# W_q in four loads of strided rows and x in two loads, in a decode kernel that streams its K and V caches

## The chip, the cores and the metric

The kernel runs on one core of one Trainium2 chip. The metric is the device time of one execution in microseconds (us). The kernel before takes 659.33 us, the median of 3 runs (659.29 to 659.46).

## What is computed

One decode step of two sequences: a pre-normalised attention block with cached keys and values, and then a gated feed-forward block. All inputs are bf16. Cut to what matters:

```python
B, Sq, D = 2, 1, 512
Hq, Hkv, Sk, Dh = 32, 32, 8192, 128        # F = 1376

def _A_ref(x, k_cache, v_cache, wq, wo):
    q = (x @ wq).reshape(B, Sq, Hq, Dh).transpose(0, 2, 1, 3)
    scores = jnp.einsum("bhqd,bhkd->bhqk", q, k_cache) * (Dh ** -0.5)
    p = _softmax(scores, axis=-1)
    o = jnp.einsum("bhqk,bhkd->bhqd", p, v_cache)
    return o.transpose(0, 2, 1, 3).reshape(B, Sq, Hq * Dh) @ wo

h = x + _A_ref(_layernorm(x), k_cache, v_cache, wq, wo)
h2 = h + _B_ref(_layernorm(h), W_gate, W_up, W_down)
```

K and V are 134 MB each. W_q is 512 x 4096, 4.2 MB. Each x row has 512 values, 1 KB.

## The kernel before

The caches come from HBM as tiles of 128 partitions x 64 KB (8.4 MB). One tile holds four heads of one sequence, with 32 partitions to a head. There are three such buffers (`bufs`). Steps 0 to 14 each take one K tile and one V tile; the last four heads are taken in two steps of half tiles.

A step runs in this order. PE transposes the last 16 to 32 columns of 128 keys (L349) and multiplies them with q (L340). DVE multiplies the rest of the K tile with q (`products`, L375) and adds the products up (`scores`, L393 and L395). ACT takes the exponentials (L415), DVE places them (L420), and PE multiplies them with the V tile (`values`, L446).

The order of all instructions is written out by hand, engine by engine (`tc.manual_schedule`). All large loads are issued by SP, in program order, on one queue; each load into a buffer waits until its old contents have been read. The V tile of step i+1 takes the buffer of step i's K tile, so SP issues it when DVE has finished the scores of step i. The K tile of step i+2 takes the buffer of step i's V tile, so SP issues it when PE has finished its values.

At the start, ACT issues the loads of x (L190) into two partitions of buffer 2, and SP issues W_q (L193) into the first half of the same buffer, where a partition holds four rows of W_q (32 KB). Then SP issues the K and V tiles of step 0 into buffers 0 and 1 (L165, in `load_tile`). Meanwhile POOL fills constants. PE transposes x (L238), `ln_cols` normalises it (L172 to L185), and PE multiplies it with W_q (L252). DVE copies the product into buffer 2 (L255), and PE and ACT spread q over the partitions (L259 to L276). When buffer 2 has been read for the last time (L267), SP issues the K tile of step 1 into it (L279, through L165).

Semaphores of loads are handed out in turn from a set of eight; the loads of x, W_q and the first K and V tile are eight in all.

After the steps come the output projection with W_o (L502 and L509), and the feed-forward block with W_gate and W_up (L686) and W_down (L719). Their loads are the last in SP's queue (L567 to L621), among them three loads of 32 rows of W_down (L616).

Of the kernel before, what the change touches and what calls it, by code (L numbers as in the profile page):

```python
# [13 lines left out]
def _free(t, offset, dims):  # L14

    return bass.AP(tensor=t.tensor, offset=t.offset + offset, ap=[t.ap[0]] + [list(d) for d in dims])


def _dram(t, offset, dims):
    return bass.AP(tensor=t.tensor, offset=t.offset + offset, ap=[list(d) for d in dims])  # L20
# [3 lines left out]
def kernel(  # L24
# [13 lines left out]
    nc = tc.nc  # L38
    P = nc.NUM_PARTITIONS
    B, Sq, D = A_x.shape  # L40
    _, Hkv, Sk, Dh = A_k_cache.shape
    Hq = A_wq.shape[1] // Dh
    F = B_W_gate.shape[1]
    KC = D // P
# [10 lines left out]
    HALF = TILE // 2  # L55
# [36 lines left out]
    bufs = [big.tile([P, TILE], bf16, name=f"tile{k}") for k in range(3)]  # L92
# [67 lines left out]
    def load_tile(cache, s, dst, pieces=1):  # L160
        h = NH * s.g + (0 if s.quad else 2 * s.k)
        n = s.nt * Dh
        w = n // pieces
        for k in range(pieces):
            nc.sync.dma_start(  # L165
                out=dst[:, k * w:(k + 1) * w], in_=_dram(cache, (s.b * Hkv + h) * Sk * Dh + k * w, [[n, P], [1, w]]),
            )

    def ln_cols(src, dst_bkc, pfx):

        m_ps = ps.tile([P, B, KC], f32, tag="mx")
        nc.tensor.matmul(out=m_ps, lhsT=mean_w, rhs=src, start=True, stop=True)  # L172
        mean = small.tile([P, B], f32, tag=pfx + "mean")
        nc.vector.tensor_reduce(out=mean, in_=m_ps, axis=AXIS.X, op=ALU.add)
        dev = small.tile([P, B, KC], f32, tag=pfx + "dev")
        nc.vector.tensor_tensor(out=dev, in0=src, in1=_free(mean, 0, [[1, B], [0, KC]]), op=ALU.subtract)
        sq = small.tile([P, B, KC], f32, tag=pfx + "sq")
        nc.vector.tensor_tensor(out=sq, in0=dev, in1=dev, op=ALU.mult)
        v_ps = ps.tile([P, B, KC], f32, tag="mx")
        nc.tensor.matmul(out=v_ps, lhsT=mean_w, rhs=sq, start=True, stop=True)  # L180
        rstd = small.tile([P, B], f32, tag=pfx + "rstd")
        nc.vector.tensor_reduce(out=rstd, in_=v_ps, axis=AXIS.X, op=ALU.add)
        nc.scalar.activation(out=rstd, in_=rstd, func=ACT.Sqrt, bias=eps_col, scale=1.0)
        nc.vector.reciprocal(out=rstd, in_=rstd)
        nc.vector.tensor_tensor(out=dst_bkc, in0=dev, in1=_free(rstd, 0, [[1, B], [0, KC]]), op=ALU.mult)  # L185

    with tc.manual_schedule():

        for b, k, n in ((0, 0, 2), (0, 2, 2), (1, 0, 2), (1, 2, 1), (1, 3, 1)):
            nc.scalar.dma_start(  # L190
                out=xr[b:b + 1, k * P:(k + n) * P], in_=_dram(A_x, b * D + k * P, [[D, 1], [1, n * P]]),
            )
        nc.sync.dma_start(out=bufs[2][:, 0:HALF], in_=_dram(A_wq, 0, [[KC * Hq * Dh, P], [1, KC * Hq * Dh]]))  # L193
        load_tile(A_k_cache, steps[0], steps[0].kt)
        load_tile(A_v_cache, steps[0], steps[0].vt)

# [5 lines left out]
            out=nscale, in_=nscale, compare_op=ALU.not_equal, fill=-SCALE,  # L202
# [5 lines left out]
            out=ident_f, in_=ident_f, compare_op=ALU.not_equal, fill=1.0,  # L208
# [4 lines left out]
            out=sel, in_=sel, compare_op=ALU.not_equal, fill=1.0,  # L213
# [9 lines left out]
            out=pick, in_=pick, compare_op=ALU.not_equal, fill=1.0,  # L223
# [15 lines left out]
        nc.vector.tensor_copy(xc, x_ps.rearrange("p c b -> p b c"))  # L239
        xn = small.tile([P, KC, B], bf16, tag="xn")  # L240
        ln_cols(xc, xn.rearrange("p c b -> p b c"), "l1")
        for r in SROWS:
            nc.vector.tensor_reduce(out=rest[r], in_=_free(ident, 0, [[1, r], [r, P // r]]), axis=AXIS.X, op=ALU.max)
# [4 lines left out]
        for g0 in range(0, NQ, 4):  # L248
            for n0 in range(NH * g0 * Dh, NH * (g0 + 4) * Dh, 4 * Dh):
                q_ps = ps2.tile([B, 4 * Dh], f32, tag="o")  # L250
                for c in range(KC):
                    nc.tensor.matmul(  # L252
                        out=q_ps, lhsT=xn[:, c, :], rhs=wq_sb[:, c, n0:n0 + 4 * Dh], start=(c == 0), stop=(c == KC - 1),
                    )
                nc.vector.tensor_copy(qrow[:, n0:n0 + 4 * Dh], q_ps)  # L255
            for b in range(B):
                r_ps = ps2.tile([P, 4, Dh], f32, tag="tp")
                for j in range(NH):
                    nc.tensor.matmul(  # L259
                        out=r_ps[j * (P // NH):(j + 1) * (P // NH)], lhsT=sel[:, b, 0:P // NH],  # L260
# [5 lines left out]
        for j in range(2):  # L266
            nc.tensor.matmul(  # L267
                out=r_ps[j * (P // 2):(j + 1) * (P // 2)], lhsT=sel[:, B - 1, :],
# [318 lines left out]
        for k in range(1, len(SETS)):  # L587
# [3 lines left out]
            out=wo[:, (HM + 1) * D:Hq * D], in_=_dram(A_wo, (HM + 1) * Dh * D, [[P // 4 * D, 4], [D, P // 4], [1, D]]),  # L591
# [19 lines left out]
        for w, src in ((0, B_W_gate), (1, B_W_up)):  # L611
            nc.sync.dma_start(
                out=wgu[:, w].rearrange("p c f -> p (c f)"), in_=_dram(src, 0, [[KC * F, P], [1, KC * F]]),
            )
        for q0 in range(AGAIN, P, AGAIN):
            nc.sync.dma_start(  # L616
                out=wd_sb[q0:q0 + AGAIN, FC - 1, :], in_=_dram(B_W_down, (F - P + q0) * D, [[D, AGAIN], [1, D]]),
            )
        for f0, n in FSETS[:-1]:
# [10 lines left out]
            out=z2_ps, lhsT=ones, rhs=_free(zc, ((B - 1) * NQ + groups[Q][1]) * NH, [[1, nb]]), start=True, stop=True,  # L630
# [63 lines left out]
        for c in range(KC):  # L694
            nc.tensor.transpose(hT_ps[:, c, :], hb[:, c].rearrange("p k b -> p (k b)"), ident)
        nc.scalar.activation(
            out=hrow.rearrange("q (p c) -> q p c", c=KC), in_=hT_ps.rearrange("q c p -> q p c"), func=ACT.Copy,
# [9 lines left out]
            out=gate, in0=g_ps, scalar=0.0, in1=_free(rvar, 0, [[0, FC], [1, B]]), op0=ALU.max, op1=ALU.mult,  # L707
# [59 lines left out]
```

## Time and profile before

| | |
|---|---|
| median of 3 runs | 659.33 us (659.29 to 659.46) |
| profiled execution, first to last instruction (span) | 657.5 us |
| busy: PE, DVE, ACT, POOL | 352.1, 558.1, 123.6, 24.1 us |
| moved by DMA | 281.37 MB, mean 428 GB/s |
| x issued, used by PE | 0.74 to 2.38 us, 15.17 us |
| W_q issued, landed | 0.74 us, 12.94 us |
| q: first matmul, last read | 18.56 us, 30.96 us |
| first DVE product of steps 0 and 1 | 32.41 us, 72.48 us |

The profiled execution's own time is known by its span alone; the median of the runs lies 1.8 us above that span. The profile shows 40 equal slices of the span, with the busy share of each engine in tenths. The chain of waits is followed back from the last instruction: each line is a start, a duration and what was waited for. A load in it counts from its issue to its landing, and so includes the time it spent in the queue behind other loads. The trace also holds one record per DMA packet, with its queue, start, duration and size: a row of a tile is one packet, and each DMA engine closes its share of a load with a semaphore packet of 4 bytes. SP's loads are queue 1 and ACT's are queue 10.

### The profile page before, as it was taken

The numbers are of one execution on the slowest core, as the hardware profiler recorded it, in microseconds if no ns is written. First come the engines' busy times: TensorE is split into PE (matmuls) and PEld (weight loads), VectorE is DVE, ScalarE is ACT, GpSimd is POOL, SyncE is SP. The second block draws the span as 40 slices with busy tenths as digits, with TensorE's granted clock in tenths as the row PEclk, the third lists the DMA queues.
The fourth block names the chain that finished last, engine by engine and source line by source line (L and its number), as shares of the span: only waits on it lengthen the run. The fifth ranks groups of instructions, "written<-read, shape, count | busy, mean of one in ns | idle before, by whom it ended". The sixth has DMA issues, their size and how long they took to land.

```text
span 657.5 us, 5117 instructions
## 1 busy us (share of the span) xinstructions
PE 352.1 (54%) x2118; PEld 158.9 (24%) x2118; DVE 558.1 (85%) x252; ACT 123.6 (19%) x337; POOL 24.1 (4%) x36
## 2 busy tenths in 40 slices
PE   0730934809175380926539092552918458291997
PEld 0310311304022130312204031220403224030456
DVE  0599697988979799897979989796997969999982
ACT  0230030200203020030301103030210304201870
POOL 3080000000000000000000000000000000000020
PEclk9975775958778596877959687695968869686895
DMA  9999999999999999999999999999999999999997
GB/s 383 447 444 447 387 440 443 447 399 444 439 443 436 419 436 435 439 439 436 423 443 424 439 440 427 447 416 443 439 423 440 423 443 436 423 444 413 425 425 291
DMA packets 6948, 281.37 MB, mean 428 GB/s; under 512 B 809, under 2 KB 1422, under 8 KB 1934
## 3 DMA queue, kind: packets, MB, share of 16 engines
q1 hardware_dynamic: 6916, 281.06, 99.1%
q8 instruction: 16, 0.26, 0.1%
q14 instruction: 6, 0.05, 0.0%
q10 hardware_dynamic: 10, 0.00, 0.0%
HBM read 281.05 MB, written 0.00 MB: 427 GB/s over the span
## 4 chain that ended last, share of the span: by engine, by line
DVE 42%; DMA 37%; PE 18%; ACT 1%; issue 1%; ACTq 0%; SPq 0%; DVEq 0%
DMA tile<-in_A_k_cache_dram 30%; DVE tile L375 19%; DVE tile L393 18%; PE pv_ps L446 16%; DMA tile<-in_A_wo_dram 4%; DVE scol L395 2%; DMA tile<-in_A_x_dram 2%; DMA tile<-in_B_W_down_dram 1%; PE q_ps L252 1%; DVE pgq L420 1%; ACT ecol L415 1%; DVE pm L399 1%; DVE qrep L395 0%; DVE pm L410 0%; DVE hmax L412 0%
## 5 line engine op out<-in xcount | busy, mean ns | idle before, releaser
L446 PE MATMUL pv_ps<-tile,pgq 128*16 128x512 bf16 x960 | 244.3, 421 | 235.8 <-DVE pgq L420 223.2
L375 DVE TENSOR_TENSOR tile<-tile,qrep 128x29696 bf16<-128x29696 bf16 (+3 forms) x16 | 232.4, 14524 | 44.9 <-DMA tile<-in_A_k_cache_dram 44.9
L393 DVE TENSOR_TENSOR tile<-tile 128x14848 bf16<-128x14848 bf16 (+7 forms) x68 | 236.4, 3477 | 2.2
L446 PEld LDWEIGHTS <-pgq 128*16 128x16 bf16 x960 | 91.6, 97 | 378.1 <-DVE pgq L420 234.5
L451 ACT ACTIVATE pv<-pv_ps 16x512 f32<-16x512 f32 (+1 forms) x16 | 9.4, 589 | 243.7 <-PE pv_ps L446 243.6
L350 ACT ACTIVATE tile<-t_ps 128x1024 bf16<-128x1024 bf16 x53 | 52.6, 1022 | 12.6 <-PE t_ps L349 12.1
L415 ACT ACTIVATE ecol<-scol,nmax 128x256 bf16<-128x256 f32 x14 | 7.1, 508 | 196.1 <-DVE nmax L414 196.1
L340 PE MATMUL row_ps<-tile,qz 128*24 128x512 bf16 (+1 forms) x98 | 30.1, 389 | 18.0 <-ACT tile L350 17.9
L349 PE MATMUL t_ps<-ident,tile 128*128 128x128 bf16 x424 | 32.3, 229 | 13.0 <-DMA tile<-in_A_k_cache_dram 13.0
L349 PEld LDWEIGHTS <-tile 128*128 128x128 bf16 x424 | 25.8, 103 | 28.1 <-issue 14.2
L395 DVE TENSOR_REDUCE scol<-tile 128x232 f32<-128x1856 bf16 (+1 forms) x14 | 28.9, 2067 | 0.5
L641 POOL TENSOR_TENSOR tile<-ident 6x2 bf16<-6x2 bf16 x1 | 2.1, 2147 | 583.5 <-ACT tile L381 583.5
L420 DVE TENSOR_TENSOR pgq<-ecol,ownb 128x1024 bf16<-128x1024 bf16 x15 | 10.4, 692 | 10.3 <-ACT ecol L415 10.3
L381 ACT ACTIVATE tile<-tile 128x128 bf16<-128x128 bf16 x60 | 17.6, 293 | 1.9 <-DVE tile L375 1.9
L281 POOL COPY qzp<-qTs 128x4 bf16<-128x4 bf16 x1 | 15.0, 14982 | 26.1 <-DVE qTs L276 26.1
L375 DVE TENSOR_TENSOR tile<-tile,qpair 128x4096 bf16<-128x4096 bf16 (+3 forms) x4 | 15.5, 3883 | 0.0
L340 PEld LDWEIGHTS <-qz 128*24 128x24 bf16 (+1 forms) x98 | 7.9, 92 | 27.6 <-issue 22.7
L239 DVE CAST xc<-x_ps 128x8 f32<-128x8 bf16 x1 | 0.2, 167 | 15.5 <-PE x_ps L238 15.5
L367 ACT ACTIVATE scol<-sc_ps 32x24 f32<-32x24 f32 (+1 forms) x56 | 11.7, 209 | 7.7 <-PE sc_ps L362 7.2
L362 PE MATMUL sc_ps<-ident_f,tile 24*128 24x24 f32 (+2 forms) x68 | 7.2, 220 | 11.1 <-ACT tile L358 11.1
L358 ACT ACTIVATE tile<-row_ps 24x512 f32<-24x512 f32 (+2 forms) x17 | 10.0, 586 | 13.5 <-PE row_ps L340 13.5
L381 ACT ACTIVATION_READ_ACCUMULATOR tile<-tile 128x1 f32 x60 | 11.2, 186 | 0.0
(133 smaller groups left out, 143.8 us busy)
## 6 DMA issues: line engine op xcount, KB each, us to landing
tile<-in_A_k_cache_dram SPq DMA_DIRECT2D x2, 4096.0 KB
tile<-in_A_v_cache_dram SPq DMA_DIRECT2D x2, 4096.0 KB, 19.6
tile<-in_A_wq_dram SPq DMA_DIRECT2D x1, 4096.0 KB, 12.2
tile<-in_A_wo_dram SPq DMA_DIRECT2D x1, 2048.0 KB
tile<-in_B_W_gate_dram SPq DMA_DIRECT2D x1, 1376.0 KB, 22.8
tile<-in_B_W_up_dram SPq DMA_DIRECT2D x1, 1376.0 KB
tile<-in_A_wo_dram SPq DMA_DIRECT2D x1, 1024.0 KB, 23.8
tile<-in_B_W_down_dram SPq DMA_DIRECT2D x1, 640.0 KB
```

The costliest lines, as they stand in the source:

```text
L281: nc.gpsimd.tensor_copy(qzp[:, :, 6:8], qTs[:, B - 1, Hq - NH:Hq].rearrange("p (k j) -> p k j", j=2),)
L340: nc.tensor.matmul(out=row_ps, lhsT=z, rhs=s.kt[:, (nv + c0 + k) * Dh:(nv + c0 + k + 4) * Dh], start=(u == 0), stop=(u == U - 1),)
L349: nc.tensor.transpose(t_ps[:, k, :], s.kt[:, t * Dh:(t + 1) * Dh], ident)
L350: nc.scalar.activation(out=s.kt[:, (nv + c0) * Dh:(nv + c0 + TPC) * Dh], in_=t_ps.rearrange("p t s -> p (t s)"), func=ACT.Copy,)
L367: nc.scalar.activation(out=scols[s.i][r, nv:s.nt].rearrange("p (u t) -> p t u", t=4), in_=sc_ps[r, :, :, j], func=ACT.Copy,)
L375: nc.vector.tensor_tensor(out=kv, in0=kv, in1=_free(s.qr, 0, [[0, n], [1, Dh]]), op=ALU.mult)
L381: nc.scalar.activation(out=kv, in_=kv, func=ACT.Copy, accum_out=scols[s.i][:, t:t + 1])
L393: nc.vector.tensor_tensor(out=lo, in0=lo, in1=hi, op=ALU.add)
L395: nc.vector.tensor_reduce(out=scol[:, s.na:s.nv], in_=_free(s.kt, s.na * Dh, [[Dh, s.nv - s.na], [1, 8]]), axis=AXIS.X, op=ALU.add,)
L415: nc.scalar.activation(out=ecol, in_=scols[s.i], func=ACT.Exp, scale=SCALE, bias=nmax, accum_out=zs[:, s.b, s.g:s.g + 1],)
L420: nc.vector.tensor_tensor(out=s.pg, in0=_free(ecol, 0, [[VG, s.nt // VG], [0, NH], [1, VG]]), in1=_free(ownb, 0, [[0, s.nt // VG], [VG, NH ...
L446: nc.tensor.matmul(out=pv_ps[s.i][r, :], lhsT=s.pg[:, u].rearrange("p j t -> p (j t)"), rhs=s.vt[:, u * VG * Dh:(u + 1) * VG * Dh], start= ...
```

## The change

W_q is loaded by four DMAs on SP's queue in place of one: every eighth partition from 0, every eighth from 4, every fourth from 2, and every second from 1, so 16, 16, 32 and 64 of the 128 partitions. Each partition still receives its 32 KB from the same place. x is loaded by two DMAs of a whole row (1 KB) in place of five of 512 or 256 bytes. The loads ahead of step 1 stay eight in number. Behind the first edit all lines of the kernel move down by ten or eleven.

```diff
+    def load_rows(w, dst, r0, step):
+
+        part, width = dst.ap[0][0], dst.ap[1][1]
+        nc.sync.dma_start(
+            out=bass.AP(
+                tensor=dst.tensor, offset=dst.offset + r0 * part, ap=[[step * part, P // step], [1, width]],
+            ),
+            in_=_dram(w, r0 * width, [[step * width, P // step], [1, width]]),
+        )
+
@@
-        for b, k, n in ((0, 0, 2), (0, 2, 2), (1, 0, 2), (1, 2, 1), (1, 3, 1)):
+        for b, k, n in ((0, 0, KC), (1, 0, KC)):
             nc.scalar.dma_start(
                 out=xr[b:b + 1, k * P:(k + n) * P], in_=_dram(A_x, b * D + k * P, [[D, 1], [1, n * P]]),
             )
-        nc.sync.dma_start(out=bufs[2][:, 0:HALF], in_=_dram(A_wq, 0, [[KC * Hq * Dh, P], [1, KC * Hq * Dh]]))
+        for r0, step in ((0, 8), (4, 8), (2, 4), (1, 2)):
+            load_rows(A_wq, bufs[2][:, 0:HALF], r0, step)
         load_tile(A_k_cache, steps[0], steps[0].kt)
```

## The prediction

> **What bounds the kernel now.** I read the page's busy slices and queues first, then busy time by stage, then the chain of waits at the start, then the timeline around the first K tile.
>
> The page, slices of the span and queues:
>
> ```profile
> DMA  9999999999999999999999999999999999999997
> ...
> q1 hardware_dynamic: 6916, 281.06, 99.1%
> ...
> tile<-in_A_wq_dram SPq DMA_DIRECT2D x1, 4096.0 KB, 12.2
> ```
>
> The 16 DMA engines are busy in every slice; DVE, the busiest compute engine, only 85%. W_q lands 12.2 us after its issue at 0.74, at 12.94. Busy time by stage (the last two columns are the share of the DMA engines and GB/s):
>
> ```profile
> 32.00:72.50 40.50, 11.89 (x61) 5.29 (x59) 33.53 (x13) 6.45 (x13) 14.98 (x1) 0.58 0.96 415
> 72.50:150.00 77.50, 38.58 (x192) 16.07 (x191) 69.00 (x23) 11.50 (x24) 0.00 (x0) 0.72 1.00 433
> 150.00:612.00 462.00, 249.49 (x1251) 106.70 (x1250) 416.40 (x147) 75.33 (x163) 0.00 (x0) 0.76 1.00 433
> ```
>
> From 72.5 to 612 the share is 1.00 at 433 GB/s: the loads are the bound, and compute follows. The chain of waits from 0 to 73 us (start, duration, what):
>
> ```profile
> 2.11 12.96 DMA tile<-in_A_x_dram
> ...
> 18.56 5.23 PE q_ps L252 x16
> ...
> 25.15 3.62 PE q_ps L252 x16
> ...
> 30.96 41.50 DMA tile<-in_A_k_cache_dram
> ...
> 72.48 15.64 DVE tile L375
> ```
>
> Read by its word, x is 13 us late, q follows, and K1's load (the second K tile) hangs on q. But K1 takes 41.50 us from issue to landing, while 8.39 MB at 433 GB/s take 19.4. It was issued into a queue that still held K0 and V0. So its issue was early, and its landing is set by what lies ahead in the queue. The timeline at K0's landing:
>
> ```profile
> 32.30 0.77 PEld L349 LDWEIGHTS <-tile 128*128 128x128 bf16 x8 [0.29 <-DMA tile<-in_A_k_cache_dram]
> ...
> 32.41 15.08 DVE L375 TENSOR_TENSOR tile<-tile,qrep 128x28672 bf16<-128x28672 bf16 x1
> ```
>
> PE waits for K0, although q is done: even the first step is no later than its K tile.
>
> The packet records of the trace say why x is late. Each W_q row of 32 KB is one packet of 1.213 us (27.0 GB/s) on one engine; the first 16 start at 1.78 to 2.58 and take 1.24 to 2.21. Each x load is two packets, data and semaphore (queue 10 has 10 packets). The first pair goes at 1.64 and 1.66; the next data packet goes at 6.17, and from there each x packet waits for one row to pass: 7.40, 8.62, 9.85, 11.07, 12.29, then 12.30, and the last at 14.73, after one K0 row of 2.418. PE starts on x at 15.17.
>
> **The change, part by part.**
>
> *x by two loads.* Four packets instead of ten. The first two should still go at 1.64 and 1.66, the third by 6.17 and the fourth one row later, by 7.40. With today's 0.44 from there to PE (14.73 to 15.17) x is usable by 7.84 instead of 15.17. The layernorm takes 18.56 - 15.17 = 3.39: xn by 11.23. ACT's last x issue begins at 1.29 instead of 2.11, so the table load behind it (L233) comes 0.8 earlier; the activation after that waits for POOL until 6.50 as before.
>
> *q.* Now W_q is late, at 12.94. PE's order of instructions has four W_q semaphores at L252's first pair (L263 in the changed kernel) in place of one; nothing but q is queued behind it. q starts at about 13.0 instead of 18.56: 5.5 earlier. Its 12.40 us (18.56 to 30.96) end at 25.4, where SP issues K1. What hides this: K0's rows keep the engines until 31.3 to 31.9 and V0's for 8 x 2.418 = 19.3 more, to about 51, so K1's issue at 30.96 had 20 us of cover and gets 26. DVE's first product waits for K0 at 32.30 instead of starting at 32.41: 0.1 gained, and lost again when DVE waits for K1 at 72.48 (5.5 us idle there by the waits of DVE). V1's load, released by DVE at 64.47, still comes 8 us before the queue needs it. POOL's copy L281 moves earlier; its result is read after 607 us. Worth on the end: 0.
>
> *W_q by four loads.* The same 128 rows, 8 on each engine, in pieces of 1, 1, 2 and 4 rows. Three more semaphore packets per engine, 0.009 us each: +0.03. On SP three more issues of about 0.45 (0.74 to 1.19) put K0's issue at 2.5 and V0's at 3.0; the engines need K0 at 12.0, so 9.5 us hide them. Without that cover it would be 1.35. The number of loads ahead of K1 stays eight, so the later loads keep their semaphores.
>
> What is on the path is only the end of the W_q stage (its last packets at 12.00 to 12.62), because no engine idles from there to 654. Each microsecond there moves K0, V0 and all else. Below: all engines start at 1.64, with the first x packet, instead of at up to 2.58: -0.9. Above: pieces that start as slowly as the first rows, which is a rival. I take 0, since the second piece is issued at 1.19, 0.45 behind the first, and even with the longest wait from issue to first packet (0.74 to 2.58) lies ready at 3.03, before the first row ends anywhere (3.54).
>
> **Sum.** Span 657.5 + 0.03 - 0 = 657.6. The median of 659.33 lies 1.8 above the profiled span: **659.4 us**. The forecast's own range is 658.5 to 660.3, the 0.9 of the start to either side.
>
> **Rivals.**
>
> 1. *Rows of a piece share a path into SBUF* (slower). A piece touches partitions 0, 8, ..., 120 only. If two engines then write through one path, each W_q row takes up to 1.213 longer: 8 x 1.213 = 9.7, 669.0; at half that, 664.2. It decides from the first row on that takes over 1.213 after start-up. Against: the only loads in the trace with fewer than 128 rows, L616's 32-row loads, again two rows to an engine. From 647.4 to 648.3 us 35 of their 1 KB packets took 46 ns each, just as the 128-row loads' 1 KB packets did, and the 20 packets of 11 KB beside them 413 ns each, with no stretch. These are small packets, so the case stays open: 0.14. [...]
>
> 2. *Each piece starts anew* (slower). The first rows take up to 2.21, 1.0 over the steady 1.213, and 0.65 on average. If three more pieces pay that: +1.9 to +3.0, 661.3 to 662.4. Against: K0's first row follows W_q's semaphore within 0.01 us (12.00, 12.01) at the steady 2.418. 0.10. [...]
>
> 3. *The chain taken at its word* (faster): 5.5 us less in front of K1, 653.8. Against: the queue above. 0.06.
>
> 4. *x is no earlier*, because its second load is held up in some other way. q starts as now, K0's landing still matches it: about 659.4. 0.04.
>
> **How the numbers follow.** 0.2% is 1.3 us, about what a measurement of this kernel can tell from no change. Forecast 0.66: 0.58 within 0.2%, and, since the trace has no second start to bound the 0.9 with, 0.05 faster than that and 0.03 slower. Same: 0.58 + 0.04 = 0.62. Slower: 0.03 + 0.14 + 0.10 = 0.27. Faster: 0.05 + 0.06 = 0.11. The range takes in the forecast, the fourth and second rivals and the first up to half its price: 658.4 to 664.2. It leaves out the third, the fast tail, and the dear half of the first.
>
> **What would show it.** In the changed kernel's profile: queue 10 with 4 packets and queue 1 with 6916 + 48 = 6964; x_ps by 7.9 (if at 15, rival 4); q from 13.0; K1's issue near 25.4, with some 47 us to landing; DVE's first product still at 32.3 and its second at 72.5. Rivals 1 and 2 show in the same places: W_q's landing past 13, a first slice below today's 383 GB/s, and DVE's first two products later by one and the same amount. Rival 3 would show K1 landing well before 72. I am wrong if the first product moves by over 1.3 us, or if it stays and the end moves.

## The result, and the profile after

The changed kernel takes 661.26 us (median of 8 runs, 660.99 to 661.36), against 659.36 for the kernel before in the same series (8 runs). The ratio is 1.0028, with a 95% interval of 1.0019 to 1.0038: 1.9 us slower. The profiled span went from 657.5 to 659.4.

The page of the changed kernel, the same rows as before and queue 10:

```profile
DMA  9999999999999999999999999999999999999997
GB/s 318 445 442 445 429 403 446 437 445 435 417 429 442 433 438 441 413 441 426 441 441 438 417 445 414 445 442 433 425 446 415 441 438 429 434 438 408 430 422 293
...
q1 hardware_dynamic: 6964, 281.06, 99.0%
...
q10 hardware_dynamic: 4, 0.00, 0.0%
...
tile<-in_A_wq_dram SPq DMA_DIRECT2D x1, 2048.0 KB, 12.7
```

The packet counts are as expected (6964 and 4). The row of GB/s before the change:

```profile
GB/s 383 447 444 447 387 440 443 447 399 444 439 443 436 419 436 435 439 439 436 423 443 424 439 440 427 447 416 443 439 423 440 423 443 436 423 444 413 425 425 291
```

The first slice moves 318 GB/s where it moved 383; the slices behind it are as full as they were. The busy digits do not tell, 9 in the first slice of both: a DMA engine whose packet takes twice as long is just as busy. W_q's last and largest load, issued at 2.67, lands 12.7 later. The chain of waits (start, duration, what):

```profile
2.67 12.67 DMA tile<-in_A_wq_dram
...
15.47 5.29 PE q_ps L263 x16
...
27.93 46.75 DMA tile<-in_A_k_cache_dram
```

x has gone from its head. W_q lands at 15.34 instead of 12.94, and q starts at 15.47, 3.1 earlier than the 18.56 of before. The second K tile's load is issued at 27.93, 3.0 earlier, and yet lands later: 27.93 + 46.75 = 74.68, against 72.46. The timeline at the first K tile:

```profile
34.68 1.57 PE L360 MATMUL t_ps<-ident,tile 128*128 128x128 bf16 x13 [5.50 <-DMA tile<-in_A_k_cache_dram]
34.74 15.09 DVE L386 TENSOR_TENSOR tile<-tile,qrep 128x28672 bf16<-128x28672 bf16 x1 [5.33 <-DMA tile<-in_A_k_cache_dram]
```

PE and DVE now stand idle for over 5 us before K0 (the brackets: idle time before, and what ended it). DVE's first product comes at 34.74 instead of 32.41, 2.33 late, and its second at 74.70, 2.22 late. So the loss is made before K0 begins. Busy time from 0 to 8 us (last column GB/s), before the change and after it:

```profile
0.00:8.00 8.00, 0.00 (x0) 0.00 (x0) 0.00 (x0) 1.49 (x2) 5.41 (x33) 1.00 0.84 328
```

```profile
0.00:8.00 8.00, 1.30 (x8) 1.16 (x8) 0.67 (x4) 1.49 (x2) 5.43 (x33) 1.00 0.80 197
```

197 GB/s in place of 328. The view counts a packet's bytes where it starts, so short windows round, but this is no rounding. The packet records give it row by row. Each of the 16 engines moves eight W_q rows, one after the other (medians over the engines, us):

| row of an engine | 1 | 2 | 3 | 4 to 8 | last end |
|---|---|---|---|---|---|
| before, start of the first engine | 1.78 | 3.54 | 4.74 | | 12.62 |
| before, took | 1.87 | 1.211 | 1.213 | 1.213 | |
| after, start of the first engine | 2.15 | 4.18 | 6.54 | | 14.86 |
| after, took | 2.30 | 2.358 | 1.63 | 1.213 | |

The first two rows are the two loads of every eighth partition. The second row takes 2.358, twice the 1.213 that W_q rows take elsewhere, on all engines alike (2.33 and up). Row 3, the first of the load of every fourth partition, begins while other engines still are at row 2, and takes 1.63. From row 4 on, in the loads of every fourth and every second partition, the rate is what it was; row 5, the first of the fourth load, takes 1.213 like the rows behind it. The W_q stage ends 2.24 late: 0.37 by a later first packet, and most of the rest by rows 1 and 2. In the five runs below that leave W_q's load as it was, the stage ends at 12.44 to 12.72, so 14.86 is no scatter.

### The profile page after: what moved, and what is told of

The parts are those of the page before. It is cut to its first block, busy times and chain, and to the rows that moved or that the text cites. A ratio compares the mean times of both kernels' runs of the same rounds, so it can differ in the third digit from the quotient of the medians.

```text
span 659.4 us, 5120 instructions
## 1 busy us (share of the span) xinstructions
PE 348.3 (53%) x2118; PEld 158.4 (24%) x2118; DVE 558.2 (85%) x252; ACT 123.4 (19%) x337; POOL 9.6 (1%) x36
## 3 DMA queue, kind: packets, MB, share of 16 engines
q1 hardware_dynamic: 6964, 281.06, 99.0%
## 4 chain that ended last, share of the span: by engine, by line
DVE 42%; DMA 38%; PE 16%; ACT 2%; issue 1%; SPq 0%; ACTq 0%; DVEq 0%
DMA tile<-in_A_k_cache_dram 31%; DVE tile L386 19%; DVE tile L404 18%; PE pv_ps L457 15%; DMA tile<-in_A_wo_dram 4%; DVE scol L406 2%; DMA tile<-in_A_wq_dram 2%; DMA tile<-in_B_W_down_dram 1%; PE q_ps L263 1%; ACT tile L392 1%; DVE pgq L431 1%; ACT ecol L426 1%; DVE pm L410 1%; DVE qrep L406 0%; DVE pm L421 0%
## 5 line engine op out<-in xcount | busy, mean ns | idle before, releaser
L457 PE MATMUL pv_ps<-tile,pgq 128*16 128x512 bf16 x960 | 239.7, 415 | 237.9 <-DVE pgq L431 226.2
L266 DVE CAST tile<-q_ps 2x512 bf16<-2x512 f32 x8 | 5.4, 678 | 10.2 <-PE q_ps L263 10.2
L263 PE MATMUL q_ps<-tile,xn 128*2 128x512 bf16 x32 | 9.0, 437 | 7.3 <-DMA tile<-in_A_wq_dram 7.3
## 6 DMA issues: line engine op xcount, KB each, us to landing
tile<-in_A_wq_dram SPq DMA_DIRECT2D x1, 2048.0 KB, 12.7
```

What stands on the lines that cost most here:

```text
L263: nc.tensor.matmul(out=q_ps, lhsT=xn[:, c, :], rhs=wq_sb[:, c, n0:n0 + 4 * Dh], start=(c == 0), stop=(c == KC - 1),)
L457: nc.tensor.matmul(out=pv_ps[s.i][r, :], lhsT=s.pg[:, u].rearrange("p j t -> p (j t)"), rhs=s.vt[:, u * VG * Dh:(u + 1) * VG * Dh], start= ...
```

## The experiments

Two theories from the prediction stood against each other: rows of a piece share a path into SBUF (path theory), and each load starts anew (start theory). A third came with the trace: the 16 rows of a small load lie 256 KB apart in HBM and collide there (HBM theory). The path is a supposition: the traces show how long a row takes, not what lies between an engine and a partition.

**Four loads of 32 rows.** The number of loads is kept, and the partitions are spread over every fourth. By the path theory these rows take 1.213 us, as row 4 of the changed kernel does on such partitions; by the HBM theory, at 128 KB from row to row, up to what row 2 took there:

```diff
-        for r0, step in ((0, 8), (4, 8), (2, 4), (1, 2)):
+        for r0, step in ((0, 4), (2, 4), (1, 4), (3, 4)):
```

> W_q again by four loads and x by two, but each W_q load takes 32 rows, every fourth from 0, 2, 1 and 3. [...] Start theory (each further load starts slowly, whatever its rows): as the change, last packets near 14.8, 661.3. [...]

Measured: 659.51 us, ratio to before 1.0004 (0.9995 to 1.0013). No difference can be told. The first 8 us again:

```profile
0.00:8.00 8.00, 1.30 (x8) 1.15 (x8) 0.67 (x4) 1.49 (x2) 5.43 (x33) 1.00 0.82 324
```

324 GB/s; rows 2 to 8 take 1.213 to 1.24, and W_q's last packet ends at 12.91. Neither four loads nor x by two costs what the change cost; the start theory falls. This run too begins with a strided load, and against it the changed kernel's W_q stage ends 14.86 - 12.91 = 1.95 later: that much is due to which partitions a load takes.

**Loads of neighbouring rows.** Sizes as in the change, partitions side by side. Here and below `load_rows` is also given the number of rows (`n`) and, where they differ from the SBUF side, the first row and the step in HBM (`s0`, `sstep`); that part of the edits is not shown:

```diff
-        for r0, step in ((0, 8), (4, 8), (2, 4), (1, 2)):
-            load_rows(A_wq, bufs[2][:, 0:HALF], r0, step)
+        for r0, n in ((0, 16), (16, 16), (32, 32), (64, 64)):
+            load_rows(A_wq, bufs[2][:, 0:HALF], r0, 1, n)
```

> The four W_q loads of 16, 16, 32 and 64 rows take neighbouring rows (0 to 15, 16 to 31, 32 to 63, 64 to 127) in place of strided ones; x by two loads. Path theory, if paths belong to groups of neighbouring partitions: 16 neighbours reach fewer paths than 16 spread ones, so the rows of the first two loads take longer than the 2.36 us they take in the changed kernel, and the time is well above 661.3; if the sharing goes with a multiple of eight instead, neighbours are free of it and the time is 659.4. HBM theory: rows are 32 KB apart as in the one load before, 659.4. Start theory: 661.3.

Measured: 672.76 us, ratio 1.0205 (1.0192 to 1.0219). The windows from 0 to 16 us (last column GB/s):

```profile
0.00:8.00 8.00, 0.00 (x0) 0.00 (x1) 0.00 (x0) 1.49 (x2) 5.42 (x33) 1.00 1.03 131
8.00:16.00 8.00, 1.45 (x8) 1.21 (x8) 2.90 (x15) 1.78 (x3) 0.00 (x0) 1.00 0.86 156
```

The DMA share reads 1.03 beside 131 GB/s: the engines are fully occupied and move less than a third of their 433. Row 2, of the load of partitions 16 to 31, takes 4.49 us, 3.7 times 1.213. The rows of the loads of 32 and 64 neighbours take 2.4 to 2.6 once running, twice. W_q ends at 26.36. So the time of a row goes with the partitions of its load: 3.7 times 1.213 on 16 neighbours, about twice on 32 or 64 neighbours, as on every eighth partition (2.358). The HBM theory, which expected 659.4, falls here already.

**Other places in HBM.** The SBUF side as in the change, the HBM side in blocks:

```diff
-        for r0, step in ((0, 8), (4, 8), (2, 4), (1, 2)):
-            load_rows(A_wq, bufs[2][:, 0:HALF], r0, step)
+        for r0, step, s0 in ((0, 8, 0), (4, 8, 16), (2, 4, 32), (1, 2, 64)):
+            load_rows(A_wq, bufs[2][:, 0:HALF], r0, step, s0=s0, sstep=1)
```

> As the changed kernel on the SBUF side (every eighth partition from 0 and from 4, every fourth from 2, every second from 1), but the rows are read from neighbouring places of W_q in HBM (rows 0 to 15, 16 to 31, 32 to 63, 64 to 127), so W_q's rows are permuted and q is not the reference's. Path theory: unchanged, rows of the first two loads 2.36 us, 661.3. HBM theory: rows at 1.213 us, 659.4. Start theory: 661.3.

Measured: 660.84 us, ratio 1.0024 (1.0015 to 1.0034). Row 2 takes 2.37, as in the changed kernel. With other HBM addresses and the same partitions, the loss stays. Its loads read the same places in HBM as those of the run with neighbouring rows, and there row 2 took 4.49: only the partitions differ.

**The first K tile by eighths.** The suspected cost on a larger tile, far from the start:

```diff
-        load_tile(A_k_cache, steps[0], steps[0].kt)
+        for r0 in range(8):
+            load_rows(A_k_cache, steps[0].kt, r0, 8)
```

> The kernel before (W_q by one load, x by five), with the first K tile by eight loads of every eighth partition, 16 rows of 64 KB each, in place of one of 128. Path theory: each of a DMA engine's 8 rows takes 4.84 us in place of 2.418, so 19.3 us more, 678.7. HBM theory: also slow, since the rows of a load lie 512 KB apart. Start theory: these loads lie in the queue long before their turn, so 659.4 to 660.

Measured: 680.32 us (one run), 21 more than before. The tile's rows take 4.3 to 5.1, mostly 5.1, in place of 2.418; 4.84 had been expected, and so 1.6 us less in the time. From 16 to 32 us:

```profile
16.00:32.00 16.00, 11.00 (x47) 4.33 (x48) 7.28 (x22) 2.87 (x5) 0.00 (x0) 1.00 1.00 205
```

A full share, at 205 GB/s. The effect has nothing to do with the start of the kernel, and it grows with the number of rows.

**16 rows on every fourth partition.** Is it the number of rows, or the partitions? Every fourth partition from 32 to 95 is 16 rows as well. If the number of rows decides, these four loads are slow; if the partitions do, the two blocks of 32 neighbours are, by the run with neighbouring rows:

```diff
-        load_tile(A_k_cache, steps[0], steps[0].kt)
+        for j in range(4):
+            load_rows(A_k_cache, steps[0].kt, 32 + j, 4, 16)
+        load_rows(A_k_cache, steps[0].kt, 0, 1, 32)
+        load_rows(A_k_cache, steps[0].kt, 96, 1, 32)
```

> The kernel before, with the first K tile by six loads: four of 16 rows each, every fourth partition from 32, 33, 34 and 35 (up to 95), and two of 32 neighbouring rows (0 to 31, 96 to 127). [...] If only the 128-row form is fast, 679.

Measured: 669.75 us (one run). The rows of the four 16-row loads take 2.418 to 2.43, at full rate; those of the two blocks of 32 neighbours 4.2 to 5.1. The windows of the one and of the other:

```profile
12.00:21.00 9.00, 3.94 (x14) 1.94 (x15) 3.48 (x16) 1.78 (x3) 0.00 (x0) 1.00 1.06 459
21.00:40.00 19.00, 9.66 (x61) 3.76 (x59) 5.24 (x10) 2.65 (x6) 0.19 (x1) 0.83 1.04 221
```

It is the partitions, not the number of rows or loads. The two blocks lie in different halves of the 128 partitions and are issued one behind the other, and the 19 us from 21 on still move only 221 GB/s.

Over these runs a row took 3.7 times its time in the 128-row load on 16 neighbouring partitions (4.49 against 1.213), about twice on 32 or 64 neighbours (2.4 to 2.6; 4.2 to 5.1 against 2.418) and on every eighth partition (2.358; mostly 5.1), and once on every second (1.213) and every fourth (1.213 to 1.24; 2.418 to 2.43). What in the chip makes it so, no run shows.

**x alone, W_q alone.** The first is the kernel before with only x's loads changed, the second the changed kernel with x's five loads put back:

```diff
-        for b, k, n in ((0, 0, 2), (0, 2, 2), (1, 0, 2), (1, 2, 1), (1, 3, 1)):
+        for b, k, n in ((0, 0, KC), (1, 0, KC)):
```

> The kernel before with only x changed: two loads of a whole row in place of five, W_q by its one load of 128 rows. All theories: the W_q stage stays as it was (last packets at 12.0 to 12.7) and the time is 659.3 within 0.5. If each x packet waits for one W_q row, as before, x's last packet comes at 7.4 and q starts at W_q's landing near 13.0, 5.5 us earlier than before, with nothing gained at the end. If x's part of the change costs anything, the time is over 660.

> Only W_q changed: the four strided loads of the changed kernel, with x by five loads as before. Path theory: the rows of the first two loads take 2.36 us each, W_q's last packets come at 14.5 to 14.9, and the time is 661.3 as with the whole change. If the loss came from the two parts together (x's row of 1 KB between the first W_q rows), it is below 660.3.

Measured: x alone 659.47 us, ratio 1.0003 (0.9994 to 1.0012); W_q alone 661.67, ratio 1.0035 (1.0021 to 1.0049). The whole loss belongs to W_q. W_q alone, from 0 to 8 us:

```profile
0.00:8.00 8.00, 0.00 (x0) 0.00 (x0) 0.00 (x0) 1.49 (x2) 5.41 (x33) 1.00 0.80 197
```

Row 2 takes 2.38 there. Its last W_q packet ends at 15.09, a little past the 14.5 to 14.9 expected, and the run lies 2.4 above its kernel before where the whole change lies 1.9 above; this half microsecond was not followed up. The chain of x alone:

```profile
0.74 12.07 DMA tile<-in_A_wq_dram
...
12.86 5.14 PE q_ps L252 x16
...
25.17 47.13 DMA tile<-in_A_k_cache_dram
...
72.43 15.64 DVE tile L375
```

This is the picture that the prediction drew for the whole change: q starts 5.7 earlier than before, K1 is issued 5.8 earlier, and DVE's second product comes at 72.43 instead of 72.48. Its first comes at 32.20 instead of 32.41.

**Short packets.** The prediction held against the path theory that L616's 32-row loads showed no stretch. These two runs keep that form up for a whole tile, in four loads of 32 neighbouring partitions and in one load of 128:

```diff
+    def load_short(w, dst, r0, n):
+
+        part, width = dst.ap[0][0], dst.ap[1][1]
+        nc.sync.dma_start(
+            out=bass.AP(
+                tensor=dst.tensor, offset=dst.offset + r0 * part,
+                ap=[[part, n], [512, width // 512], [1, 512]],
+            ),
+            in_=_dram(w, r0 * width, [[width, n], [1024, width // 512], [1, 512]]),
+        )
...
-        load_tile(A_k_cache, steps[0], steps[0].kt)
+        for r0 in range(0, P, 32):
+            load_short(A_k_cache, steps[0].kt, r0, 32)
```

The second has one `load_short(A_k_cache, steps[0].kt, 0, P)` in place of the four.

> The kernel before, with the first K tile by four loads of 32 neighbouring partitions, each 64 KB row in 64 packets of 1 KB. (The packets are every second KB of HBM over two rows' length, so step 0 works on other keys than the reference's.) This is the form of L616's loads, which showed 46 ns a packet, but kept up for a whole tile. Path theory with long and short packets alike: two engines share a path of 27 GB/s, so a 1 KB packet takes at least 2 x 1024 / 27.1 = 76 ns, and the tile 8 x 64 x 0.076 = 38.7 us in place of 19.3: 679 or more. If short packets do not share: 46 ns each, 23.6 us, 663.6.

> [...] All theories: 46 ns a packet as in L589's and L590's loads, the tile 8 x 64 x 0.046 = 23.6 us in place of 19.3, 663.6. [...]

Measured: 680.57 us with four loads of 32 partitions, 661.36 with one of 128 (one run each). With four the median packet takes 84 ns and the packets of an engine start 80 ns apart; with one, each takes 46 and they start 43 apart, so I had overrated the price of short packets by 2.2 us. From 13 to 52 us with four loads:

```profile
13.00:52.00 39.00, 13.96 (x74) 5.73 (x74) 8.71 (x25) 4.43 (x9) 0.19 (x1) 0.75 1.10 206
```

So short packets on 32 neighbours take nearly twice as long (84 against 46 ns), like long ones. But not at once: of the tile's 8192 packets 204 take under 50 ns, all in its first 0.9 us, and the first stretched one comes 0.72 us behind the first. That is 13 packets of 1 KB for each engine on average, but not a fixed number: the engines begin this tile between 11.97 and 12.45, and all show the stretch from about 12.7 to 12.8 on, the earliest after 17 packets and the latest after 7 or 8. L616's loads give an engine six.

**Two loads of 64 rows.**

```diff
-        for r0, step in ((0, 8), (4, 8), (2, 4), (1, 2)):
+        for r0, step in ((0, 2), (1, 2)):
```

> As the changed kernel, but W_q by two loads of 64 rows, every second from 0 and from 1, and x by two. [...] So far the first W_q packet came at 2.10 to 2.15 where the first load takes strided partitions, and at 1.75 to 1.78 where it takes neighbours; if the stride is the reason, it is 2.1 here too, W_q's last packets come at 12.3 to 13.0 and the time is 659.3 to 659.8. If the number of loads were the reason, it is 1.76.

Measured: 659.78 us, ratio 1.0008 (0.9999 to 1.0017); W_q's first packet at 2.08, its last end at 12.82. As expected of a strided first load. None of these versions beats the kernel before, and no run shortened the way of the queue, which stays full from W_q's first row to the last loads.

## Why the prediction was right and wrong

- **The bound.** Right. The loads set the end, and q's path does not: x alone brings q 5.7 us forward and gains nothing that can be told. The warning that the chain's word is not to be taken (third rival) holds.
- **x.** Right in direction, and it came sooner than the bound of 7.84. In the changed kernel x's second packet pair passes at 4.38 and 4.48, between the first and second W_q rows of its engine: by the times, the only W_q packet that takes its turn between the two is a semaphore packet of the first load, not a whole row. PE starts on x at 5.75. By the waits it then waited for POOL's constants (L239), no longer for x. In x alone, with W_q in one load, the pair passes at 6.34 and 7.59, close to the 6.17 and 7.40 that the prediction had worked out.
- **q's cover.** Right. What failed in its numbers is W_q's landing: q started at 15.47, not at 13.0, and K1 was issued at 27.93, not at 25.4.
- **The W_q stage.** Here the prediction failed: "I take 0". The stage ended 2.24 later. Some 1.95 of it are the rows on every eighth partition (against the run with four loads of 32 rows; the second row of each engine took 2.358 in place of 1.211); the sum put that at nothing. The rest is a term it did not have: a strided first load's first packet comes 0.37 later, and in that same run, which starts almost as late, the stage ends 0.29 late. The likeliest case, no change within 0.2%, did not happen; the first rival did. By the prediction's own sign, "I am wrong if the first product moves by over 1.3 us", its forecast of 659.4 was wrong: that product moved by 2.33. The signs of the first two rivals all came (W_q's landing at 15.34, a first slice of 318 GB/s, the first two products later by 2.33 and 2.22). The measured time lies in the range only because the range was drawn to the second rival and to half the price of the first.
- **The first rival's price.** That rows of such a piece go slower was right, the size was not; a shared path as the reason fits the rows' times but was not shown. It was priced at 4.8 to 9.7, as if all eight rows of an engine were slow. But "a piece touches partitions 0, 8, ..., 120 only" holds for the first two pieces alone; on every fourth and every second partition the rows took 1.213 from row 4 on. Two rows at twice the time are 2 x 1.213 = 2.4 more. Some of that was there already, since the first row takes 1.87 at the start in any case, and a later first packet adds 0.37.
- **Its chance of 0.14.** Too low, for a misread row. L616's packets "with no stretch" were taken as a sign that engines do not share paths. In the run with short packets in four loads even the engines that begin last pass 7 or 8 packets of 1 KB unstretched before the durations grow. Six could not be expected to show it. That they were small was said, but not what it was worth.
- **The second rival.** Wrong as a cause: four loads of 32 rows cost nothing that can be told. That the measured 661.26 meets the lower end of its price, 661.3, is chance. No cost of a further start shows in row 5 above, the first of the fourth load, at 1.213. On SP the four issues took 0.57 to 0.62 us each, not 0.45, and K0's issue came at 3.30 in place of 2.5, still far ahead of its first row at 14.51.
- **From 2.24 to 1.9.** 0.3 us are given back between 72 and 150 us. There the 64 KB rows of the profiled execution before took 0.37 us per engine above 2.418 each, and those of the changed kernel 0.06. The other traces go the same way: 0.39 to 0.54 in the three where W_q was not slowed (four loads of 32 rows, x alone, two loads of 64 rows), 0.06 in W_q alone and with other places in HBM. What slows these rows when W_q comes early was not tried and stays open.

## What to carry to other kernels

When a load is cut into pieces by partition, note for each piece which partitions it holds before counting its bytes: here loads kept the 16 DMA engines busy and moved 205 GB/s (share 1.00) or 131 GB/s (share 1.03) in place of 433, and only GB/s, or the time of a single packet, told them from full ones. In this kernel, whose load queue never runs dry, 1.9 of 2.24 us lost there went to the end, while 5.7 us won for q, which waits for those loads, were worth nothing (659.47 us with x alone). A row of a trace is evidence only for loads long enough to show the effect.

## What the hardware showed unexpectedly

- By their times, x's packets take turns with W_q's rows on one DMA engine, one packet against one row: in the kernel before, most of its ten x packets went 1.21 to 1.23 us apart, beside W_q rows of 1.213, and the last 2.43 behind the one before it, after a K0 row of 64 KB (2.418). They needed 13 us, from 1.64 to 14.73.
- A load whose partitions are strided takes SP 0.56 to 0.63 us to issue as the first one, against 0.38 to 0.40 for neighbours, and its first packet comes at 2.08 to 2.15 instead of 1.75 to 1.78. This held in all five runs with a strided first load and in the seven others; its reason was not looked for.
- The rows that go at about half the rate take 1.94 times the usual time in the changed kernel's second row (2.358 against 1.213), but mostly 2.1 times in W_q's blocks of neighbours (2.57) and in the K tile (5.1 against 2.418). Why it is not twice in all stays open.
- Four loads of 32 rows of every fourth partition run at full rate (rows 2 to 8 in 1.213 to 1.24), while the rows of the load of 32 neighbours took 2.4 to 2.6. How the rows are dealt out to the engines, no run here shows.
